# Two V tiles of a decode kernel loaded as 112 rows and two times 8 rows

## The chip, the core and the metric

The kernel runs on one core of a Trainium2 chip. The metric is the time of one execution on the device in microseconds (us). Three runs of the kernel before gave 1982.34, 1982.47 and 1984.11 us, median 1982.47 us.

## What is computed

The reference is one decode step through four attention layers. The token is a row `x` of 640 numbers. Each layer normalises `x`, multiplies it by `wq` to get 32 query heads of 192 numbers, scores every head against 8192 cached keys, takes the softmax, sums the 8192 cached values with it, multiplies the result by `wo` and adds it to `x`. Layers one and three use the caches and weights of set A, layers two and four those of set B. All data are bfloat16.

```
scores = einsum("bhqd,bhkd->bhqk", q, k_cache) * (Dh ** -0.5)
p = softmax(scores);  o = einsum("bhqk,bhkd->bhqd", p, v_cache)
x = x + o.reshape(B, Sq, H * Dh) @ wo
```

Each cache holds 32 x 8192 x 192 numbers, about 100 MB, and there is one query row for all of it: nearly all the work is to bring K and V in once per layer.

## The kernel before

**Tiles.** Heads are taken two at a time, as 16 pairs `p` per layer (index `l` from 0, so layers two and four are `l` = 1 and 3). The K or V of one pair is laid over 128 partitions, each with 128 cached rows of 192 numbers: 49,152 bytes in a partition, 6144 KB in a tile. `pool` has eight slots of half a tile (`TS` elements per partition). A transfer that `whole` (L210) allows fills two neighbouring slots with one `dma_start` (L379); others fill one slot (L381), and the last V of layers two and four comes as a half and two quarters (L374, L375).

**Compute.** For each pair, `products` (L589) lets VectorE multiply K by the query in place (L599, four pieces per half) and TensorE sum the products with a held identity matrix (L612). `softmax` (L616) reduces, finds the maximum and takes the exponential. `values` (L641) lets TensorE sum V with the probabilities (L678) into `OY`; L664 is the wait for the V tile. `gather` (L688) collects the sums on VectorE (L696, L697) and TensorE (L710). At the end of a layer the last V, `gather`, and the projection by `wo` (`project`, L531, or `project_row`, L563) must be through before the next layer's query can be formed.

**Order.** The program is written out by hand: `steps` is the order of the compute, `plan` the order of the loads. All large loads are issued by the sync engine (SP), in the order of `plan`, on one queue. `ahead` (L404) issues the next load as soon as the steps that free its slot are written down; on the chip SP then waits for the semaphore of that step, and so an issue waits for the compute that empties its slot. Each slot has a semaphore, which a landed transfer raises by 16; `need` (L396) gives the event to wait for. A wait on an engine's own list that is already covered by an earlier one is left out (`Queue.wait`, L22).

**Around the change.** In layer two the V tile of pair index 11 is the transfer issued at 855.92 us of the profiled execution, behind a K tile issued at 850.79 us and ahead of the K tile issued at 864.85 us. In layer four the V tile of index 11 is issued at 1809.76 us and the next K tile at 1826.66 us.

Of the kernel before, what the change touches and what calls it, by code (L numbers as in the profile page):

```python
# [61 lines left out]


PAIRS_W = 5
NSLOT = 8
KEPT = {0: {("k", 0)}, 1: {("v", 14), ("v", 15)}}


def build(nc, A_x, A_k, A_v, A_wq, A_wo, B_x, B_k, B_v, B_wq, B_wo, out):
    _, H, SK, DH = A_k.shape  # L70
    D = A_x.shape[-1]
    P = 128
# [13 lines left out]
    TS = JU * DH  # L86
# [11 lines left out]
    with ExitStack() as ctx:  # L98
# [6 lines left out]
        def sem(name):  # L105
            return ctx.enter_context(nc.semaphore(name))

        ident = sb("ident", [P, P], BF16)
        pool = sb("pool", [P, NSLOT * TS], BF16)
# [57 lines left out]
        PE = Queue(sem("pPE"))  # L167
# [2 lines left out]
        PO = Queue(sem("pPOOL"))  # L170
        SP = Queue()
        semS = [sem(f"semS{i}") for i in range(NSLOT)]
        semOL, semOE, semOB, semVQ, semX, semOUT = [sem(n) for n in ("semOL", "semOE", "semOB", "semVQ", "semX", "semOUT")]

        e = PO.op(lambda g: g.memset(ident[:], 0.0))
        PO.op(lambda g: g.affine_select(out=ident[:], in_=ident[:], compare_op=ALU.not_equal, fill=1.0,
# [5 lines left out]
        e = PO.op(lambda g: g.memset(mask, 0.0))  # L182
        for t in range(G):
            e = PO.op(lambda g, t=t: g.affine_select(
                out=mask, in_=mask, compare_op=ALU.not_equal, fill=1.0,
                base=-32 * t, pattern=[[-1, 2], [-2, VK]], channel_multiplier=1), e)
# [39 lines left out]
        for l in range(NL):  # L226
# [8 lines left out]
            for p in range(NPAIR):  # L235
# [17 lines left out]
                if p < NPAIR - 2:  # L253
                    if first_load("v", l, p) == (l, p):
                        plan += [("v", l, p, u) for u in range(2)]
                        if l == 2 and p == 1:
                            i = plan.index(("k", l, 1, 0))
# [4 lines left out]
                    if p + 1 in (PAIRS_W, 2 * PAIRS_W):  # L262
                        b = (p + 1) // PAIRS_W - 1
# [64 lines left out]
                    plan[i:i + 2] = [m, n]  # L328
                    turn[n[1:3]] = (1, 0)

        freed, landed = {}, {}
        issued = [0]

        def wq_rows(l, g):
# [10 lines left out]
        def transfer(n):  # L345
            l = n[1]
            o = ORDER[l]
            w = W[l % 2]
            free = [freed[b] for b in before[n]]
            if n[0] in ("wol", "woe"):  # L350
                r0 = o["wol"] * PD
                a, b = (0, OI) if l < 3 else (0, OI - 1) if n[0] == "wol" else (OI - 1, OI)
                return SP.op(lambda s: s.dma_start(
                    rows[:, a * D:b * D], w["wo"][r0:r0 + PD].rearrange("(p i) n -> p (i n)", p=P)[:, a * D:b * D]),
                    *free, sem=semOL if n[0] == "wol" else semOE, inc=16)
            if n[0] == "t":
                return max(free, key=lambda e: e[1]) if free else None
            if n[0] == "wob":
                r0 = o["wo"][2] * PD
                return SP.op(lambda s: s.dma_start(  # L360
                    slot[place[("wo", l, 2)]][:, (NW - NB[l]) * D:NW * D],
                    w["wo"][r0:r0 + PAIRS_W * PD].rearrange("(p i) n -> p (i n)", p=P)[:, (NW - NB[l]) * D:]),
                    sem=semOB, inc=16)
            if n[0] == "vq":
                n = ("v", l, NPAIR - 1, 1)
            i = place[n]
            t = slot[i]
            if n[0] in "kv":
                h = 2 * pair(l, n[2])
                r = w[n[0]][0, h:h + 2].rearrange("h (p j) d -> (h p) (j d)", j=J)  # L370
                if quarters(n):
                    x = TS // 2
                    if n in landed:
                        return SP.op(lambda s: s.dma_start(t[:, x:], r[:, TS + x:]), sem=semVQ, inc=16)  # L374
                    return SP.op(lambda s: s.dma_start(t[:, 0:x], r[:, TS:TS + x]), *free, sem=semS[i], inc=16)  # L375
                if whole(*n[:3]):
                    if n[3] == 1:
                        return landed[n[:3] + (0,)]
                    f = lambda s: s.dma_start(pool[:, i * TS:(i + 2) * TS], r)  # L379
                else:  # L380
                    f = lambda s: s.dma_start(t, r[:, n[3] * TS:(n[3] + 1) * TS])  # L381
            elif n[0] == "wq" and l < 2:
                f = lambda s: s.dma_start(pool[:, i * TS:i * TS + DC * QW], w["wq"].rearrange("(p c) n -> p (c n)", c=DC))
            elif n[0] == "wq":
                c0, k = Q_PARTS[n[2]]
                f = lambda s: s.dma_start(
                    wq_rows(l, n[2]),
                    w["wq"][:, o["q1"] * PD:o["q1"] * PD + QC].rearrange("(p c) n -> p c n", c=DC)[:, c0:c0 + k, :])
            else:
                r0 = o["wo"][n[2]] * PD  # L390
                k = NW - NB[l] if n[2] == 2 else NW
                f = lambda s: s.dma_start(
                    t[:, 0:k * D], w["wo"][r0:r0 + PAIRS_W * PD].rearrange("(p i) n -> p (i n)", p=P)[:, 0:k * D])
            return SP.op(f, *free, sem=semS[i], inc=16)

        def need(n):  # L396

            while n not in landed:
                m = plan[issued[0]]
                issued[0] += 1  # L400
                landed[m] = transfer(m)
            return landed[n]
# [45 lines left out]
        def layer(l, ev_z, ev_true):  # L448
# [7 lines left out]
            if l == 2:  # L456
                busy(2)
            e = DV.op(lambda v: v.scalar_tensor_tensor(out=nv[:], in0=mv[:, 0:1], scalar=mv[:, 0:1], in1=mv[:, 1:2],
                                                       op0=ALU.mult, op1=ALU.subtract))
            e = DV.op(lambda v: v.tensor_scalar(vs[:], nv[:], -float(DH), float(DH) * EPS, ALU.mult, ALU.add), e, last["rs"])  # L460
# [6 lines left out]
            if l < 2:  # L467
                e = need(("wq", l, 0))
# [4 lines left out]
            else:  # L473
                e = ev_first[l - 2]
# [166 lines left out]
            def values(p, us=(0, 1)):  # L641

                par = (l * NPAIR + p) % 2
                nl, np_ = first_load("v", l, p)
                k = 2 if p == NPAIR - 1 else VK
                N = min(512, k * DH)
                PE.wait(ev_p[p])
                if 0 in us:
                    PE.wait(last["rl"])
                    if p < NPAIR - 1:  # L650
                        e = PE.op(lambda t: t.matmul(TB[96:97, C_L:C_L + 2], lhsT=ones[:, 0:1], rhs=l_col[par][:],  # L651
                                                     start=True, stop=True), bank=TBu)
                    else:
                        for h in range(2):
                            e = PE.op(lambda t, h=h: t.matmul(TB[64 * h:64 * h + 64, C_L:C_L + 1], lhsT=ones[:, 0:1].broadcast_to([P, 64]),
                                                              rhs=l_col[par][:, h:h + 1], start=True, stop=True),
                                      signal=h == 1, bank=TBu)
                    last["lc"][par] = ev_l[p] = e
                PE.wait(last["O"])
                rounds = J // k // G  # L660
                for r in range(us[0] * rounds // 2, (us[-1] + 1) * rounds // 2):
                    u, i = divmod(r, rounds // 2)
                    u = turn[nl, np_][u]
                    PE.wait(need(("v", nl, np_, u)))  # L664
                    t = slot[place[("v", nl, np_, u)]]
                    if p == NPAIR - 1 and i == rounds // 4 and quarters(("v", nl, np_, u)):
                        if l == 3:
                            busy(6)
                        PE.wait(need(("vq", l)))
                    for c in range(k * DH // N):  # L670
                        for g in range(G):
                            j = (i * G + g) * k
                            o, x, y = (O[32 * g:32 * g + 2 * k, c * N:(c + 1) * N],
                                       p_sb[par][:, u * JU + j:u * JU + j + k, :].rearrange("p j h -> p (j h)"),
                                       t[:, j * DH + c * N:j * DH + (c + 1) * N])
                            f, fin = r == 0, r == rounds - 1
                            e = PE.op(lambda t, c=c, g=g, o=o, x=x, y=y, f=f, fin=fin: (
                                t.matmul(o, lhsT=x, rhs=y, start=f, stop=fin) if c == 0 else  # L678
                                matmul_held(t, o, x, y, f, fin, 32, 32 * g)),
                                signal=(fin and c == k * DH // N - 1 and g == G - 1), bank=Ou)  # L680
                if 1 not in us:
                    return
                ev_O[p] = last["p"][par] = e
                if not stays("v", l, p):
                    for u in range(2):
                        freed[("v", nl, np_, u)] = e
# [80 lines left out]
            if l + 1 == NL:  # L767
                a = slot[place[("wo", 3, 2)]][0:33, 0:HD]
                return a, AC.op(lambda c: c.activation(a, YR, ACT.Copy), ev_y, last["oT"], bank=YBu)
            ev_z = DV.op(lambda v: v.tensor_tensor(z[:], xc[:], YB[:, 0:DC], ALU.add), ev_y, ev_xc, bank=YBu)  # L770
            e = DV.op(lambda v: v.tensor_tensor(x_true[:], x_true[:], YB[:, 0:DC], ALU.add), ev_y, ev_true, bank=YBu)
# [60 lines left out]
```

## Time and profile before

| what | value |
|---|---|
| median of three runs | 1982.47 us (1982.34 to 1984.11) |
| span of the profiled execution, first to last instruction | 1982.1 us |
| bytes moved, mean rate over the span | 849.25 MB, 428 GB/s |
| DMA packets | 26,930; 12,416 of them of 49,152 bytes |
| busy: PE / DVE / ACT | 65% / 61% / 7% of the span |
| chain that ended last: DMA / DVE / PE | 67% / 17% / 15% |
| one `dma_start` at L379 on SP | 0.328 us |

The page gives no other time of the profiled execution than its span, which lies 0.4 us under the median of the runs. In the page, PE is TensorE, DVE is VectorE, ACT is ScalarE, SP is the sync engine. The core has 16 DMA engines that move the data; the DMA line gives the mean busy share of the 16 in each fortieth of the span, in tenths. A landing is told by 16 raises of its semaphore, and the trace holds the time of each raise; their spread tells how far the DMA engines are apart.

### The profile page before, as it was taken

What the parts mean: (1) busy time and instruction counts of PE and PEld (TensorE: products, weight loads), DVE (VectorE), ACT (ScalarE), POOL (GpSimd) and SP (SyncE); (2) the same over time, 40 slices, a digit from 0 to 9 for tenths busy, and PEclk for the clock granted to TensorE, in tenths of its full rate; (3) what the DMA queues carried; (4) which work ended last, traced back from release to release, by engine and by line L of the source; (5) the groups of instructions that cost most, each with busy time, mean ns of one, the idle gap of its engine ahead of it and who ended that gap; (6) DMA issues with size and microseconds to landing.
All of it is one profiled execution on the core that took longest, in us unless ns stands there. A gap on an engine that the chain in (4) does not pass through costs nothing.

```text
span 1982.1 us, 13748 instructions
## 1 busy us (share of the span) xinstructions
PE 1288.6 (65%) x8248; PEld 146.4 (7%) x3160; DVE 1201.2 (61%) x1376; ACT 139.9 (7%) x462; POOL 4.5 (0%) x23
## 2 busy tenths in 40 slices
PE   3567476666466666666785676675776766657658
PEld 0001001000100100100020010010001001000001
DVE  3566467467166657556745565665764775665656
ACT  0000000000000000000010000000000100000000
POOL 0000000000000000000000000000000000000000
PEclk9787776778677777777887877878787888777779
DMA  9999999999999999999999999999999999999998
GB/s 414 438 431 430 431 436 432 430 430 429 435 432 433 434 430 432 429 435 433 426 407 426 425 426 426 432 430 431 434 429 427 435 431 433 433 432 431 433 433 367
DMA packets 26930, 849.25 MB, mean 428 GB/s; under 512 B 3058, under 2 KB 3188, under 8 KB 3828
## 3 DMA queue, kind: packets, MB, share of 16 engines
q1 hardware_dynamic: 26724, 848.38, 99.6%
q8 instruction: 45, 0.74, 0.2%
q14 instruction: 17, 0.14, 0.0%
q10 hardware_dynamic: 144, 0.00, 0.0%
HBM read 848.36 MB, written 0.00 MB: 428 GB/s over the span
## 4 chain that ended last, share of the span: by engine, by line
DMA 67%; DVE 17%; PE 15%; ACT 1%; issue 0%; SPq 0%
DMA pool<-in_B_k_cache_dram 27%; DMA pool<-in_A_v_cache_dram 20%; DVE pool L599 15%; DMA pool<-in_A_k_cache_dram 14%; PE S L58 6%; DMA pool<-in_B_v_cache_dram 6%; PE OY L58 5%; PE OY L678 3%; DVE acc L697 1%; ACT p_sb L636 1%; DVE s_sb L621 1%; PE S L612 0%; DVE m_bf L623 0%; PE OY L538 0%; PE QM L626 0%
## 5 line engine op out<-in xcount | busy, mean ns | idle before, releaser
L599 DVE TENSOR_TENSOR pool<-pool,q_sb 128x3072 bf16<-128x3072 bf16 x512 | 861.1, 1753 | 229.5 <-DMA pool<-in_B_k_cache_dram 133.5
L58 PE MATMUL S<-pool,ident 128*128 128x512 bf16 x2944 | 789.5, 425 | 19.5 <-DVE pool L599 17.6
L710 PE MATMUL TB<-acc,small 128*1 128x192 f32 x240 | 82.7, 495 | 212.0 <-DVE acc L697 212.0
L58 PE MATMUL OY<-pool,p_sb 128*16 128x512 bf16 x1920 | 202.7, 498 | 0.0
L696 DVE TENSOR_SCALAR acc<-OY,small 128x192 f32<-128x192 f32 x64 | 26.7, 418 | 287.5 <-PE OY L58 256.3
L678 PE MATMUL OY<-pool,p_sb 128*16 128x512 bf16 (+1 forms) x1216 | 148.2, 495 | 69.5 <-DMA pool<-in_A_v_cache_dram 63.5
L612 PE MATMUL S<-pool,ident 128*128 128x512 bf16 x128 | 61.8, 483 | 201.3 <-DVE pool L599 201.2
L697 DVE SCALAR_TENSOR_TENSOR acc<-OY,small,acc 128x192 f32<-128x192 f32 x424 | 177.1, 418 | 14.9
L621 DVE TENSOR_REDUCE s_sb<-S 128x64 f32<-128x512 f32 x128 | 88.0, 688 | 69.7 <-PE S L58 69.7
L527 ACT ACTIVATE q_sb<-QM 128x192 bf16<-128x192 f32 x60 | 19.9, 331 | 944.0 <-PE QM L521 944.0
L721 ACT ACTIVATE rows<-TB,small 1x192 bf16<-1x192 f32 x120 | 43.2, 406 | 596.3 <-PE TB L710 596.3
L692 DVE RECIPROCAL small<-TB 1x2 f32<-1x2 f32 x64 | 11.2, 175 | 94.5 <-PE TB L651 75.3
L636 ACT ACTIVATE p_sb<-s_sb,small 64x128 bf16<-64x128 f32 x128 | 55.7, 435 | 161.2 <-DVE small L630 160.4
L612 PEld LDWEIGHTS S<-pool,ident 128*128 128x128 bf16 x128 | 12.9, 101 | 676.2 <-DVE pool L599 604.4
L651 PE MATMUL TB<-small,ones 128*1 128x2 f32 x120 | 11.4, 165 | 74.1 <-ACT p_sb L636 74.1
L678 PEld LDWEIGHTS OY<-pool,p_sb 128*16 128x16 bf16 (+1 forms) x1216 | 39.8, 107 | 217.3 <-issue 138.8
L626 PE MATMUL QM<-ident,m_bf 128*64 128x64 bf16 x128 | 14.0, 216 | 54.4 <-DVE m_bf L623 53.9
L710 PEld LDWEIGHTS TB<-acc,small 128*1 128x1 f32 x240 | 19.8, 101 | 310.8 <-DVE acc L697 284.0
L630 DVE TENSOR_REDUCE small<-QM 128x1 f32<-128x64 f32 x64 | 14.4, 225 | 35.2 <-PE QM L626 35.2
L521 PEld LDWEIGHTS QM<-rows,one_b 1*64 1x64 bf16 x120 | 6.2, 100 | 347.0 <-issue 341.1
L538 PE MATMUL OY<-oT,pool 128*128 128x1 bf16 x675 | 28.6, 178 | 1.9 <-ACT oT L584 1.9
L538 PEld LDWEIGHTS OY<-oT,pool 128*128 128x128 bf16 x675 | 27.8, 131 | 3.8 <-ACT oT L584 2.5
(74 smaller groups left out, 215.2 us busy)
## 6 DMA issues: line engine op xcount, KB each, us to landing
pool<-in_B_k_cache_dram SPq DMA_DIRECT2D x28, 6144.0 KB, 37.9
pool<-in_B_v_cache_dram SPq DMA_DIRECT2D x28, 6144.0 KB, 33.5
pool<-in_A_v_cache_dram SPq DMA_DIRECT2D x27, 6144.0 KB, 27.5
pool<-in_A_k_cache_dram SPq DMA_DIRECT2D x34, 3072.0 KB, 20.5
pool<-in_A_k_cache_dram SPq DMA_DIRECT2D x14, 6144.0 KB, 36.4
pool<-in_A_v_cache_dram SPq DMA_DIRECT2D x10, 3072.0 KB, 14.7
pool<-in_B_k_cache_dram SPq DMA_DIRECT2D x8, 3072.0 KB, 22.5
pool<-in_A_wo_dram SPq DMA_DIRECT2D x6, 2400.0 KB, 21.9
```

What stands on the lines that cost most here:

```text
L58: return t.add_instruction(mybir.InstMatmult(name=t.bass.get_next_instruction_name(), engine=mybir.EngineType.PE, ins=[t.lower_ap(rhs), t. ...
L527: lambda a: a.activation(q_sb[i][:], QM[:, 0:DH], ACT.Copy), e, last["q"][i], bank=QMu)
L538: e = PE.op(lambda t, i=i, c=c, f=y_first[0], fin=n[0] == "wol" and i == k - 1: t.matmul(YB[:, c:c + 1], lhsT=t3[:, i, c:D:DC], rhs=o[:, i ...
L599: e = DV.op(lambda v, d0=d0: v.tensor_tensor(k3[:, :, d0:d0 + QD], kin[:, :, d0:d0 + QD], q_sb[qi][:, d0:d0 + QD].unsqueeze(1).broadcast_t ...
L612: t.matmul(S[:, :], lhsT=ident[:], rhs=k3[:, :, d0:d0 + R], start=True, stop=fin) if d0 == 0 else
L621: lambda v, u=u: v.tensor_reduce(s[:, u * JU:(u + 1) * JU], SP_[u][:].rearrange("p (j r) -> p j r", r=R), AX.X, ALU.add), ev_S[p, u], last ...
L636: ev_p[p] = AC.op(lambda a, h=h, r=r: a.activation(p_sb[par][r, :, h], s[r, :], ACT.Exp, bias=negm[par][r, 0:1], accum_out=l_col[par][r, h ...
L678: t.matmul(o, lhsT=x, rhs=y, start=f, stop=fin) if c == 0 else
L696: v.tensor_scalar(acc[:], O[:, 0:DH], pick[:, 0:1], None, ALU.mult) if i == 0 else
L697: v.scalar_tensor_tensor(out=acc[:], in0=O[:, i * DH:(i + 1) * DH], scalar=pick[:, i:i + 1], in1=acc[:], op0=ALU.mult, op1=ALU.add)), e if ...
L710: e = PE.op(lambda t, h=h: t.matmul(TB[96:97, C_O + h * DH:C_O + (h + 1) * DH], lhsT=half[:, h:h + 1], rhs=acc[:], start=True, stop=True), ...
L721: last["TO"] = last["row_written"] = AC.op(lambda a, h=h: a.activation(orow[:, o0 + h * DH:o0 + (h + 1) * DH], TB[96:97, C_O + h * DH:C_O ...
```

## The change

In `transfer`, a whole tile that is listed in `ASIDE` no longer comes in one transfer of 128 rows. It comes as one of 112 rows (partitions 0 to 111) under the slot's semaphore, and, issued straight behind it by the same engine, two of 8 rows each (partitions 112 to 119 and 120 to 127) under a new semaphore `semA`. In `values`, TensorE waits for that semaphore too. The rows, their places and the bytes are the same. Two tiles are listed: V of pair index 11 in layers two and four.

```diff
+ASIDE = {("v", 1, 11), ("v", 3, 11)}
+ASIDE_ROWS = 16
...
-        freed, landed = {}, {}
+        freed, landed, aside = {}, {}, {}
...
                 if whole(*n[:3]):
                     if n[3] == 1:
                         return landed[n[:3] + (0,)]
-                    f = lambda s: s.dma_start(pool[:, i * TS:(i + 2) * TS], r)
+                    if n[:3] in ASIDE:
+                        a = P - ASIDE_ROWS
+                        e = SP.op(lambda s: s.dma_start(pool[0:a, i * TS:(i + 2) * TS], r[0:a]), *free, sem=semS[i], inc=16)
+                        for b in range(a, P, 8):
+                            aside[n[:3]] = SP.op(lambda s, b=b: s.dma_start(pool[b:b + 8, i * TS:(i + 2) * TS], r[b:b + 8]),
+                                                 sem=semA, inc=16)
+                        return e
+                    else:
+                        f = lambda s: s.dma_start(pool[:, i * TS:(i + 2) * TS], r)
...
-                    PE.wait(need(("v", nl, np_, u)))
+                    PE.wait(need(("v", nl, np_, u)), aside.get(("v", nl, np_)))
```

More of the change, by code (lines that the diff above doesn't have):

```diff
@@ L172, in build @@
         semS = [sem(f"semS{i}") for i in range(NSLOT)]
-        semOL, semOE, semOB, semVQ, semX, semOUT = [sem(n) for n in ("semOL", "semOE", "semOB", "semVQ", "semX", "semOUT")]
+        semOL, semOE, semOB, semVQ, semX, semOUT, semA = [
+            sem(n) for n in ("semOL", "semOE", "semOB", "semVQ", "semX", "semOUT", "semA")]
         e = PO.op(lambda g: g.memset(ident[:], 0.0))
```

## The prediction

> **What bounds the kernel.** I first read the slices of the page, its queues and the chain that ended last.
>
> ```profile
> DMA  9999999999999999999999999999999999999998
> GB/s 414 438 431 430 431 436 432 430 430 429 435 432 433 434 430 432 429 435 433 426 407 426 425 426 426 432 430 431 434 429 427 435 431 433 433 432 431 433 433 367
> ...
> q1 hardware_dynamic: 26724, 848.38, 99.6%
> q8 instruction: 45, 0.74, 0.2%
> ...
> DMA 67%; DVE 17%; PE 15%; ACT 1%; issue 0%; SPq 0%
> ```
>
> The DMA engines are busy from end to end, on one queue; the 17% and 15% of VectorE and TensorE in the chain lie beside running transfers. So time can be won only where DMA engines stand idle. The view of windows shows where: at the ends of layers two and four.
>
> ```profile
> 1002.00:1004.00 2.00, 1.72 (x24) 0.80 (x28) 0.00 (x0) 0.00 (x0) 0.00 (x0) 0.50 0.99 414
> 1004.00:1006.00 2.00, 2.00 (x31) 1.14 (x19) 0.00 (x0) 0.00 (x0) 0.00 (x0) 0.68 0.82 342
> 1006.00:1008.00 2.00, 1.72 (x43) 1.71 (x43) 0.17 (x1) 0.19 (x1) 0.00 (x0) 1.00 0.78 272
> ...
> 1972.00:1974.00 2.00, 2.00 (x26) 0.40 (x13) 0.00 (x0) 0.00 (x0) 0.00 (x0) 1.00 0.92 380
> 1974.00:1976.00 2.00, 0.88 (x18) 0.29 (x16) 0.00 (x0) 0.00 (x0) 0.00 (x0) 1.00 0.58 241
> 1976.00:1978.00 2.00, 1.77 (x23) 0.87 (x13) 0.84 (x2) 0.00 (x0) 0.00 (x0) 1.00 0.37 144
> ```
>
> The last two columns are the DMA share and GB/s. The share doesn't drop at once but over 4 to 6 us: some DMA engines have finished while others still work. The trace holds the 16 raises of a landing's semaphore, one per DMA engine. At 36 us they lie within 1.07 us. For the last V transfer of layer two the eighth engine is 2.99 us behind the first, the ninth 3.57, the last 6.35 (landed at 1009.58); in layer four 3.19, 4.13 and 6.10 (1975.38). Compute waits for the last one, as the chain shows:
>
> ```profile
> 993.05 16.54 DMA pool<-in_B_v_cache_dram
> ...
> 1937.43 37.95 DMA pool<-in_B_v_cache_dram
> ```
>
> Followed packet by packet, eight engines carry in turn the 16,384-byte packets of q8 (about 1.07 us each, 45 in the run), which fits a leading and a trailing eight. The trace doesn't number the engines.
>
> **What the change does to the load of the engines.** A row of 49,152 bytes is one packet: 12,416 such packets are 97 whole tiles of 128. A packet takes 1.82 us (trace median), so a tile costs each of the 16 engines 8 packets, 14.53 us from one tile to the next. The 112 rows can be 7 packets each, 12.7 us. A transfer of 8 rows has 8 packets, so at least eight engines get none of it. If the same eight take both, they carry 9 rows and the others 7. No transfer of before has fewer than 16 packets on q1 but the output's, so which engines these are isn't shown.
>
> **Costs beside other work.** SP issues two more transfers per listed tile, at the 328 ns of
>
> ```profile
> L379 SPq DMA_DIRECT2D pool<-in_B_v_cache_dram x28: 327/328/328, 531.1 to 1914.1; - x28
> ```
>
> that is 0.66 us before SP can wait for the next slot. Next in line is the K issue at 864.85 us, 8.9 us after 855.92; the transfer starts only after some 18 us more (first landing 897.54 minus 14.53), so the 0.66 us cost nothing. Without this cover they would cost 0.66 us each time. The added wait of TensorE at L664 stands before V's matmuls:
>
> ```profile
> 891.68 0.11 PEld L678 LDWEIGHTS OY<-pool,p_sb 128*16 128x16 bf16 x4
> ```
>
> In layer two V of index 11 has landed at 888.55 and is used at 891.68, a margin of 3.1 us (1855.12 and 1858.56 in layer four, 3.4 us). If the 8 rows land later than that, `gather` and the K issue at 896.17 move with TensorE; this issue's packets start at 912 (926.61 minus 14.53), so some 16 us of queued work cover it; in layer four the issue at 1863.07 has 30 us. So the wait by itself moves nothing; what counts is how far engines on q1 fall back.
>
> **The price of the 8-row transfers.** This is the unknown. Lower end: eight engines write eight rows side by side, 1.82 us. Upper end: eight neighbouring partitions take their rows one after another, 8 x 1.82 = 14.5 us, which is also the time in which any eight partitions get their rows in the rows of before (14.53 us a tile). Each row is near to one side of the question: the packet's is for an engine, the tile's is for a group of partitions. I see no reason to prefer one and take the middle, (1.82 + 14.53) / 2 = 8.2 us for each. The eight engines then need 12.7 + 2 x 8.2 = 29.1 us in place of 14.53, **14.5 us more**; at the ends +1.82 us, and 12.7 + 29.1 - 14.5 = +27.2 us.
>
> [...]
>
> **Forecast: slower, 2001 us.** I take the eight to be the leading ones. [...] Layer two: 0.6 + 14.5 = 15.1 in place of 6.35, +8.8 us. Layer four: 1.2 + 14.5 = 15.7 in place of 6.10, +9.6 us. The lag stays until an end of a layer, since the engines that are late always have queued work. Sum: 1982.1 + 18.4 = 2000.5 of span, and with the 0.4 us by which the median of the runs lies above it, 2001. Chance 0.60. Own range 1990 (a price of about 5.5 us per transfer: 12.7 + 11 - 14.5 = 9.2, less a lead of 5.3, is +4 each) to 2012 (the trailing eight take them, 2 x 14.5 = 29). With 14.5 us per transfer it would be +21 and +22, 2026; I give no more than 0.06 to the part above 2011.
>
> **Rival: a levelling (chance 0.25).** The 8 rows cost 1.82 us each and fall on the leading eight, which go back by one row while the trailing eight gain one. Layer two: the greater of 2.99 + 1.82 = 4.81 and 6.35 - 1.82 = 4.53, so 1.54 us are gained; layer four: 3.19 + 1.82 = 5.01 in place of 6.10, 1.09. Together 2.6 us, 1979.8: within 0.2% of the time, which is 3.96 us. This is the other side: not slower. It decides if an 8-row transfer takes less than about 3.5 us (the lead of the middle engine, 6.35 - 0.6 = 5.75 and 6.10 - 1.2 = 4.9 us, 5.3 on average, plus the spared row of 1.82 is 7.1 us for the two). For it: the two groups at 2.99 and 3.57. More than one row can't be won at either end, so 3.6 us is the limit, 1978.8.
>
> **Rival: the wrong eight (0.08).** As before, but the trailing eight take the rows: 1.82 us lost at each end, 3.6 together, 1986.1. For it: nothing in the trace names the engines.
>
> **Rival: no effect (0.07).** The rows go to the engines that would have had them anyway: two engines with four rows each per transfer. The load is as before, 1982.5.
>
> **How the numbers follow.** The likeliest is the price, 2001. About 0.2% is what a measurement of this kernel can tell from no change, so the bounds are 1978.5 and 1986.4. Faster than that needs a levelling beyond its limit, or other lags in the run: 0.04. Within: 0.21 of the levelling, 0.07 no effect, 0.05 of the wrong eight, 0.02 of a price that the lead just covers: 0.35. Slower: 0.61. The range goes from 1979 (leaving some 0.07 below) to 2011 (0.06 above).
>
> **What would show it.** Right: in the changed trace the packets of the 16 rows take far more than 1.82 us; the raises of the K tile behind (issued at 864.85) lie some 15 us apart and not 5.5; the DMA share falls off over 15 us at the end of layer two and of the run; the chain still ends on the V transfer. Wrong: packets of 1.82 us there and raises of the last V within about 5 us mean the levelling; raises 8 us apart mean the wrong eight. The forecast is wrong as well if the price is one or two rows, if half the rows fall on other engines, or if a late wait at L664 holds the queue empty.

## The result and the profile after

Four runs of the changed kernel took 2035.13, 2036.33, 2037.01 and 2040.3 us, median 2036.67; four of the kernel before on the same chip had a median of 1982.4. The ratio is 1.0276, with a 95% interval of 1.0262 to 1.0289: **slower by 54.3 us**. The profiled execution is the one of 2035.13 us; its span is 2033.3 us, 51.2 more than before.

The page of the changed kernel: DMA share in tenths, GB/s in 40 slices of 50.8 us, the queue, and the chain that ended last.

```profile
DMA  9999999999999999999999999999999999999998
GB/s 417 432 433 431 432 433 428 433 434 432 433 433 432 429 432 433 430 226 432 423 396 429 427 432 435 427 429 436 428 428 434 433 432 433 433 430 346 309 433 356
...
q1 hardware_dynamic: 26756, 848.38, 99.5%
...
DMA 61%; PE 19%; DVE 16%; another core or an unknown queue 2%; ACT 1%; issue 1%; SPq 0%
```

The rate tells where the time went: 226 in the eighteenth slice (864 to 915 us) and 346 and 309 in the 37th and 38th (1830 to 1932), against 430 or so around them. These are the two listed tiles. The DMA line above it stays at nines throughout: the engines count as busy while each packet takes longer. Two other slices are low, 396 and the last, 356; they were 407 and 367 before, and layers two and four end there.

The windows of that stretch (start and end in us, length, busy time of PE, PEld, DVE, ACT and POOL, granted clock, DMA share, GB/s), first before the change:

```profile
868.00:880.00 12.00, 5.36 (x17) 0.40 (x5) 6.37 (x5) 0.72 (x2) 0.00 (x0) 0.57 0.98 422
880.00:892.00 12.00, 9.15 (x51) 0.42 (x11) 9.39 (x10) 1.31 (x5) 0.00 (x0) 1.00 1.02 442
892.00:904.00 12.00, 5.58 (x52) 0.89 (x16) 4.32 (x10) 0.72 (x2) 0.00 (x0) 0.67 0.98 422
```

and after it:

```profile
868.00:880.00 12.00, 0.99 (x4) 0.13 (x1) 0.98 (x1) 0.72 (x2) 0.00 (x0) 0.50 1.10 246
880.00:892.00 12.00, 10.73 (x42) 0.20 (x2) 12.00 (x8) 0.00 (x0) 0.00 (x0) 0.85 0.98 217
892.00:904.00 12.00, 2.36 (x14) 0.30 (x6) 2.44 (x6) 1.31 (x5) 0.00 (x0) 0.72 1.12 172
904.00:912.00 8.00, 0.00 (x0) 0.00 (x0) 0.00 (x0) 0.00 (x0) 0.00 (x0) 0.50 0.82 166
912.00:924.00 12.00, 4.81 (x52) 0.80 (x20) 3.34 (x8) 0.36 (x2) 0.00 (x0) 0.76 0.94 393
```

The rate halves at 868.9 us, when the first DMA engine starts on the 112 rows, long before the 8-row transfers. It falls further, to 166 to 172, when these come, and is back by 915. By single packets: from 868.9 us on **all 16 engines** are slow, those still on the K tile before included. A packet of 49,152 bytes that starts between 870 and 891 us takes 3.0 to 3.8 us, most of them 3.5 to 3.8, in place of 1.82; one that starts between 891 and 910, with the 8-row transfers under way, takes 3.7 to 6.3 us. Added up over the whole run, the packets take 49.6 us longer for each of the 16 engines, out of the 51.2 us by which the span grew. So nearly all of the loss is slow packets, and at most 1.6 us are a queue left empty by the late wait, which the prediction named as one more way to be wrong. The K tile behind (issued at 863.90) lands at 929.26, against 903.08 before: 26.2 us later. Its raises are 8.59 us apart, 5.54 before.

The loss is not won back, and not enlarged, at the ends of the layers. The windows there after the change:

```profile
1028.00:1030.00 2.00, 1.37 (x32) 0.67 (x32) 0.00 (x0) 0.00 (x0) 0.00 (x0) 1.00 0.96 407
1030.00:1032.00 2.00, 1.72 (x35) 1.61 (x32) 0.17 (x1) 0.18 (x1) 0.00 (x0) 1.00 0.89 371
1032.00:1034.00 2.00, 2.00 (x51) 1.79 (x53) 0.00 (x0) 0.00 (x0) 0.00 (x0) 0.93 0.96 346
2024.00:2026.00 2.00, 2.00 (x24) 0.36 (x9) 0.00 (x0) 0.00 (x0) 0.00 (x0) 1.00 0.69 265
2026.00:2028.00 2.00, 1.55 (x20) 0.39 (x17) 0.43 (x2) 0.00 (x0) 0.00 (x0) 1.00 0.18 76
```

The last V of layer two lands at 1036.03 us (1009.58 before, +26.4) with its raises 6.51 us apart (6.35 before); that of layer four lands at 2026.62 (1975.38, +51.2) with raises 9.45 apart (6.10). So the second tile costs another 24.8 us, and all of it is still there at the end.

The chain of waits (start, us, what) has these three lines:

```profile
896.84 18.13 another core or an unknown queue
...
1889.52 17.85 another core or an unknown queue
...
1989.53 37.09 DMA pool<-in_B_v_cache_dram
```

The first two have no name, but the timeline (start, busy us, instruction, idle time before and what ended it) gives one to the first:

```profile
915.11 0.61 PE L689 MATMUL OY<-pool,p_sb 128*16 128x512 bf16 x4 [18.27 <-DMA pool<-in_B_v_cache_dram]
```

It is TensorE at the added wait for the 8 rows (the V matmuls are L689 now). Compute stands there, but the queue still has packets: the next K tile is issued at 919.14, and its own packets start only at 935 (first landing at 949.74, less 14.53). The transfers behind it are late by themselves. The third line shows that the run still ends on a V transfer.

### The profile page after: what moved, and what is told of

It reads as the page before. It is cut to its first block, busy times and chain, and to the rows that moved or that the text cites. A ratio compares the mean times of both kernels' runs of the same rounds, so it can differ in the third digit from the quotient of the medians.

```text
span 2033.3 us, 13754 instructions
## 1 busy us (share of the span) xinstructions
PE 1291.3 (64%) x8248; PEld 146.6 (7%) x3160; DVE 1201.1 (59%) x1376; ACT 139.8 (7%) x462; POOL 4.5 (0%) x23
## 4 chain that ended last, share of the span: by engine, by line
DMA 61%; PE 19%; DVE 16%; another core or an unknown queue 2%; ACT 1%; issue 1%; SPq 0%
DMA pool<-in_B_k_cache_dram 24%; DMA pool<-in_A_v_cache_dram 19%; DMA pool<-in_A_k_cache_dram 15%; DVE pool L610 13%; PE S L58 9%; PE OY L58 5%; DMA pool<-in_B_v_cache_dram 4%; PE OY L689 3%; DVE acc L708 1%; ACT p_sb L647 1%; DVE s_sb L632 1%; PE S L623 1%; PE OY L549 0%; DVE m_bf L634 0%
## 5 line engine op out<-in xcount | busy, mean ns | idle before, releaser
L58 PE MATMUL S<-pool,ident 128*128 128x512 bf16 x2944 | 789.9, 425 | 20.0 <-DVE pool L610 18.6
L689 PE MATMUL OY<-pool,p_sb 128*16 128x512 bf16 (+1 forms) x1216 | 146.8, 491 | 101.3 <-DMA pool<-in_A_v_cache_dram 59.2
L732 ACT ACTIVATE rows<-TB,small 1x192 bf16<-1x192 f32 x120 | 43.1, 405 | 628.5 <-PE TB L721 628.5
L689 PEld LDWEIGHTS OY<-pool,p_sb 128*16 128x16 bf16 (+1 forms) x1216 | 39.1, 106 | 250.9 <-issue 176.3
## 6 DMA issues: line engine op xcount, KB each, us to landing
pool<-in_A_v_cache_dram SPq DMA_DIRECT2D x10, 3072.0 KB, 15.1
```

The lines of the kernel that those rows point to most:

```text
L58: return t.add_instruction(mybir.InstMatmult(name=t.bass.get_next_instruction_name(), engine=mybir.EngineType.PE, ins=[t.lower_ap(rhs), t. ...
L732: last["TO"] = last["row_written"] = AC.op(lambda a, h=h: a.activation(orow[:, o0 + h * DH:o0 + (h + 1) * DH], TB[96:97, C_O + h * DH:C_O ...
```

## The experiments

Each diff is against the changed kernel; what differs is the list of tiles and the branch that loads them. `d` is the tile in `pool`, `r` its rows in the cache. Where a tile comes in several transfers, the first raises the slot's semaphore, the others `semA`, and TensorE waits for both, as in the change. Times are single runs, but where an interval is given; beside them stands a run of the kernel before on the same chip, or the median of 13 where 1982.49 is named. The four runs of the changed kernel lie 5 us apart, so less than that between two single runs shows nothing.

**One transfer of 16 rows.** Is it the 8-row form that costs?

```diff
-                        for b in range(a, P, 8):
-                            aside[n[:3]] = SP.op(lambda s, b=b: s.dma_start(pool[b:b + 8, i * TS:(i + 2) * TS], r[b:b + 8]),
...
+                        parts = [(a, a) for a in (slice(0, 112), slice(112, 128))]
...
+                        for a, b in parts:
+                            g = lambda s, a=a, b=b: s.dma_start(d[a], r[b])
```

The first entry of a pair is the place in the tile, the second the rows of the cache. The next experiments with several transfers of rows differ from this one in `parts` and, where it is shown, in the list of tiles.

> The 16 rows come in one transfer instead of two of 8, the 112 rows as in the change, in both tiles. [...] Theory two (the 8-row transfers are the whole cost, as the prediction had it): the 112 rows run at 1.82 us per packet and the time is within a few us of before, under 1990 us.

Measured: 2028.58 us against 1982.59, +46.0, or 23.0 per tile. The windows:

```profile
880.00:892.00 12.00, 10.23 (x39) 0.20 (x2) 12.00 (x8) 0.00 (x0) 0.00 (x0) 0.79 0.94 205
892.00:904.00 12.00, 3.08 (x17) 0.30 (x6) 3.16 (x6) 1.31 (x5) 0.00 (x0) 0.78 1.14 193
```

The rate is halved just as long. Joining the two 8-row transfers saves 4 us a tile (27.1 less 23.0), not most of the price: the price isn't that of the 8-row form alone. Theory two (under 1990 us) is out.

**Two transfers of 64 rows.** Here every engine gets 4 rows of each transfer, if rows are shared out evenly, and no transfer is small.

```diff
+                        parts = [(a, a) for a in (slice(0, 64), slice(64, 128))]
```

> The two listed tiles come as two transfers of 64 rows, partitions 0 to 63 and 64 to 127. [...] A rival theory, that only a row count that is no power of two is handled badly (112): packets of 1.82 us and no change, 1982 us.

Measured: 2025.68 us, +43.1, or 21.5 per tile. One window of its stretch:

```profile
880.00:892.00 12.00, 9.55 (x33) 0.20 (x2) 11.37 (x7) 0.00 (x0) 0.00 (x0) 0.68 0.99 213
```

Half rate through the whole tile, 3.4 to 4.4 us per packet on all 16 engines. The 1982 us expected for a row count that is a power of two did not come. It isn't an uneven number of rows per engine, on which the prediction was built. It isn't smallness either: a cut at partition 64 is enough.

**Eight neighbouring rows, or eight rows apart.** The tile of layer two alone comes in 16 transfers of 8 rows, once of neighbouring partitions, once of partitions four apart.

```diff
-ASIDE = {("v", 1, 11), ("v", 3, 11)}
+ASIDE = {("v", 1, 11)}
...
+                        parts = [(a, a) for a in [slice(b, b + 8) for b in range(0, P, 8)]]
```

for the neighbouring rows, and for those four apart

```diff
+                        parts = [(a, a) for a in [slice(h + b, h + b + 29, 4) for h in range(0, P, 32) for b in range(4)]]
```

> Layer two only: the listed tile comes as 16 transfers of 8 neighbouring rows each; layer four as in the kernel before. [...] A rival theory, that any short transfer halves the rate whatever its partitions: packets of 3.6 us, 58 us for the tile, about +38 us, near 2020 us. Engines at their own rate (1.82 us per packet, 29 us): +9 us, 1991 us.

> As the kernel with 16 transfers of 8 neighbouring rows, layer two only, but the 8 rows of a transfer lie 4 partitions apart (the same rows of the tile to the same partitions, in another order). [...] If the partitions do not matter: the same time as that kernel.

Measured: neighbouring 2033.62 us, +51.0; four apart 2016.13, +33.5, both for one tile. Windows of the neighbouring rows:

```profile
868.00:880.00 12.00, 1.44 (x4) 0.34 (x4) 0.50 (x2) 0.72 (x2) 0.00 (x0) 0.50 1.09 250
880.00:892.00 12.00, 9.70 (x37) 0.20 (x2) 11.93 (x8) 0.00 (x0) 0.00 (x0) 0.80 0.95 262
...
904.00:916.00 12.00, 0.00 (x0) 0.00 (x0) 0.00 (x0) 0.00 (x0) 0.00 (x0) 0.50 0.99 168
```

and of the rows four apart:

```profile
868.00:880.00 12.00, 5.58 (x17) 0.45 (x5) 6.39 (x5) 0.72 (x2) 0.00 (x0) 0.57 1.00 430
...
892.00:904.00 12.00, 0.00 (x0) 0.00 (x0) 0.00 (x0) 0.00 (x0) 0.00 (x0) 0.52 1.01 209
904.00:916.00 12.00, 0.00 (x0) 0.00 (x0) 0.00 (x0) 0.00 (x0) 0.00 (x0) 0.50 0.99 209
```

The 430 is the most telling figure of the study. Eight-row transfers run at full rate (1.82 us per packet) into the lower 64 partitions when their rows lie four apart, and at half rate (3.5 to 3.9 us) as soon as the same pattern goes to the upper 64. Neighbouring rows take 3.4 to 4.5 us for the first 10 us, then 2.6 to 2.9 in the lower half and 4.6 to 4.8 in the upper. Neither 2020 nor 1991 us, the times expected for them, came out; and the rows four apart took 17.5 us less than they did, so the partitions do matter. So eight rows in a transfer need not cost anything by their number; it depends on which partitions they go to. In every slow stretch the slow packets are on all 16 engines, though an 8-row transfer feeds eight: the others carry the ordinary tiles in front and behind and go just as slowly. The raises of the rows' semaphore also tell which eight these are. In the run with rows four apart, in the order in which the 16 engines end the K tile, they are the second, third, fourth, sixth, seventh, tenth, twelfth and fifteenth: five of the leading eight, three of the trailing.

With 16 short transfers, slow packets are not the whole price. The eight engines that get none of the V tile run out of work while TensorE waits for it, as the DMA share shows for the rows four apart:

```profile
916.00:928.00 12.00, 4.82 (x48) 0.60 (x16) 0.75 (x2) 0.00 (x0) 0.00 (x0) 0.56 0.58 197
```

Over the whole run (durations of all packets, divided by 16, against the span) the packets take 37.8 us longer than before with neighbouring rows and 19.4 four apart; the engines stand idle 11.9 and 12.8 us longer. So the partitions are compared by the rates and the packets, not by the whole price of a tile.

**Rows eight apart in the lower half.** As the one before, but in the lower 64 partitions the eight rows of a transfer lie 8 apart and so reach from 0 to 63. Do only rows that lie close together slow each other?

```diff
+                        parts = [(a, a) for a in [slice(b, b + 57, 8) for b in range(8)] + [slice(64 + h + b, 64 + h + b + 29, 4) for h in (0, 32) for b in range(4)]]
```

> [...]

Measured: 2029.4 us against 1982.49, +46.9, where four apart gave +33.5. In the lower half:

```profile
868.00:880.00 12.00, 1.44 (x4) 0.34 (x4) 0.63 (x2) 0.72 (x2) 0.00 (x0) 0.50 1.11 242
```

242 in place of 430 GB/s, 3.6 to 3.8 us per packet, but some of 2.1 to 3.2 between 882 and 888. Packets take 34.1 us longer in all, against 19.4 four apart. No two of the eight rows are closer than eight partitions, so it isn't only rows close together that go slowly; why those eight apart do isn't shown.

**Neighbouring partitions, rows apart in HBM.** Is it where the rows land or where they are read? The partitions are those of the neighbouring case; the cached rows are read four apart.

```diff
+                        parts = [(slice(h + 8 * b, h + 8 * b + 8), slice(h + b, h + b + 29, 4)) for h in range(0, P, 32) for b in range(4)]
```

> Layer two only: 16 transfers of 8 rows to neighbouring partitions, but their rows in HBM lie 4 apart, so 128 rows of this V tile land on other partitions than their probabilities and the sum over this tile is changed. If the partitions set the cost: as with neighbouring rows, 2034 us, packets of 2.8 us and then 4.6. If the place in HBM sets it: as with rows 4 apart, 2016 us, packets of 1.82 and then 3.8.

Measured: 2040.05 us, +57.6, against +51.0 with the rows read side by side. Windows:

```profile
868.00:880.00 12.00, 1.44 (x4) 0.34 (x4) 0.77 (x2) 0.72 (x2) 0.00 (x0) 0.53 1.09 242
...
904.00:916.00 12.00, 0.00 (x0) 0.00 (x0) 0.00 (x0) 0.00 (x0) 0.00 (x0) 0.50 1.07 168
```

Spreading the reads gains nothing; the rates are those of the neighbouring case or somewhat lower (156 against 172 GB/s from 916 to 928). The rows four apart have the same reads in the same order and differ from this kernel in the partitions alone: 2016.13 against 2040.05. The partitions decide. Whether the reads add a little to it, the 6.6 us more are too few to tell.

**The 112 rows alone.** The 8-row transfers are left out in both tiles, and with them the added wait.

```diff
-                        for b in range(a, P, 8):
...
+                        return SP.op(lambda s: s.dma_start(pool[0:a, i * TS:(i + 2) * TS], r[0:a]), *free, sem=semS[i], inc=16)
```

> Both tiles: only the 112 rows are loaded, the 16 rows of the two short transfers are left out (the sum over these tiles is changed). If the 112 rows run at half rate by themselves: about 25 us each in place of the 12.7 at full rate and 14.5 of the whole tile, +11 us per tile, near 2004 us, so that of the 54 us some 22 are due to them and 32 to the 8-row transfers. If the 112 rows are slow only because short transfers stand behind them: packets of 1.82 us and 1979 us.

Measured: 2012.91 us, +30.4, or 15.2 per tile, with an eighth of the tile's bytes gone; the 112 rows are slow by themselves. Its windows:

```profile
880.00:892.00 12.00, 10.10 (x39) 0.20 (x2) 12.00 (x8) 0.00 (x0) 0.00 (x0) 0.82 0.98 213
892.00:904.00 12.00, 3.01 (x17) 0.30 (x6) 3.09 (x6) 1.31 (x5) 0.00 (x0) 0.75 0.94 213
```

More than half of the 27.1 us per tile is the large transfer; the two small ones add the other 11.9 us, some 1.8 of it for the bytes that are missing here. An estimate comes near the 15.2: all engines are slow from the first one's entry into the tile to the last one's exit, some 7 packets and 5.4 us of spread (3 packets), so 10 packets cost 1.82 us more each, 18.2, less the 1.82 us of the row left out: 16.4.

**The same work cut by columns.** Three transfers again, with the same sizes, the same extra issues, semaphore and wait, but each spans all 128 partitions: 112, 8 and 8 of the 128 cached rows that a partition holds.

```diff
+                        for a, b in ((0, 112), (112, 120), (120, 128)):
+                            g = lambda s, a=a * DH, b=b * DH: s.dma_start(d[:, a:b], r[:, a:b])
```

> Both tiles in three transfers with the same two extra issues, the same second semaphore and the same waits as the change, but cut along the 128 numbers of rows within a partition (112, 8 and 8), so that each transfer has all 128 partitions. If the cost lies in the partitions: no change, 1982 to 1984 us, packets of 48 KB cut into 43 and 3 KB at the usual rate. If the issues, the waits or the number of transfers cost: a part of the 54 us is seen here.

Measured in three rounds: median 1983.23 us, ratio 1.0003 with an interval of 0.9994 to 1.0013. The windows, and the GB/s of the page:

```profile
880.00:892.00 12.00, 9.12 (x48) 0.44 (x11) 9.50 (x9) 1.31 (x5) 0.00 (x0) 1.00 1.02 432
892.00:904.00 12.00, 5.87 (x54) 0.84 (x20) 4.04 (x10) 0.72 (x2) 0.00 (x0) 0.67 1.00 430
```

```profile
GB/s 413 437 432 429 430 434 430 434 431 429 436 430 432 431 434 431 428 433 432 429 408 426 430 432 430 432 431 427 433 430 428 433 433 432 434 431 431 432 430 371
```

No slice is low but the first and those at the ends of layers two and four, as before. Issues, semaphore and wait cost nothing that can be measured; TensorE doesn't stand at the wait here: it is busy for 5.87 us from 892 to 904, 5.58 before, 2.36 with the change. What is left for the 54 us is the cut across partitions.

**The 112 rows in layer one.** The branch is that of the 112 rows alone. Does the price of a tile follow from how far the engines are apart? In layer one they have drifted apart less (2.3 us in the run before, against 5.5 and 5.3 at the two tiles of the change), so a tile should cost less.

```diff
-ASIDE = {("v", 1, 11), ("v", 3, 11)}
+ASIDE = {("v", 0, p) for p in range(4, 8)}
```

> Only the 112 rows are loaded, in four V tiles of layer one (index 4 to 7) instead of the two of layers two and four; their 16 rows are left out, so the sums over these tiles are changed. There the 16 DMA engines are 2.3 us apart, against some 5.4 at the tiles of the change. If all engines run at half rate from the first engine's entry into the 112 rows to the last one's exit, a tile costs (7 rows + 2.3 / 1.82 rows) x 1.82 us less the 1.82 us of the row left out, 13.2 us, four of them 53 us: near 2035 us. If the cost doesn't depend on how far the engines are apart, it is the 15.2 us per tile of the kernel with 112 rows alone: near 2043 us.

Measured: 2023.64 us against 1981.76, +41.9 for four tiles, 10.5 each. The GB/s of its page:

```profile
GB/s 414 430 431 314 293 302 433 429 433 433 433 430 434 429 433 433 431 431 431 434 403 418 430 426 432 427 429 427 430 428 425 436 431 433 432 433 431 431 433 372
```

The direction holds, the size doesn't: neither 2035 nor 2043 us. With the engines 2.3 us apart at first the packets take some 3.2 to 3.8 us at the start and end of a tile but 2.0 to 3.0 in its middle. So a 112-row transfer isn't simply at half rate: a tile cost 15.2 us in layers two and four, 10.5 in layer one. The formula above is an estimate that fits one drift; on what the price depends, these two don't show.

**The change in layer two alone.**

```diff
-ASIDE = {("v", 1, 11), ("v", 3, 11)}
+ASIDE = {("v", 1, 11)}
```

> The change in layer two only. If each tile has its own price and nothing is won back later, half of the 54 us: near 2010 us. If a part of the loss of layer two is caught up in layers three and four (queued work, or a reset of the engines' lag at the end of layer two), the price of this one tile is less than half: under 2007 us, and that of layer four is the larger one.

Measured: 2009.24 us, +27.5, half of 54.3 within the spread of single runs. The two prices add up, and a loss in layer two is neither won back nor doubled later.

## Why the prediction was wrong in size

The direction was right, and in part for the reason given: which partitions a transfer writes sets how fast its rows come, 430 GB/s with rows four apart in the lower half and 242 eight apart. Why isn't shown. The forecast was +18.6 us; measured were 54.3.

**The step that failed first: "The 112 rows can be 7 packets each, 12.7 us."** It put the large transfer at the full rate, for no other reason than that each engine gets fewer rows. The 112 rows alone cost 15.2 us per tile over a whole tile of 14.5, that is 29.7 in place of 12.7. I asked how many rows an engine has, never which partitions the transfer writes; that question was put to the 8-row transfers only.

**The second: that only the engines with the 8 rows fall back, and their lead covers some of it.** "I take the eight to be the leading ones" gave back 5.3 us on average. The eight were five of the leading and three of the trailing where they could be told, and it doesn't matter, since packets were slow on all 16 engines (3.0 to 3.8 us from 870 to 891 us): none kept its 1.82 us while the others fell back. This also speaks against the levelling, beside the measured time. The 0.6 and 1.2 us in the sums, and in the lead of 5.3, stand for the middle of the leading eight: the mean of the fourth and fifth raise of the last V before. That the eight fall back together from that point was an assumption, which no run shows; the last raises came 6.51 and 9.45 us behind the first, not 15.1 and 15.7.

**The 8-row price was near by luck.** I took 8.2 us for each, the middle of two ends between which I could not choose; the two together add 11.9, 6.0 each. That number is what the 112 rows leave of the 27.1, so it adds up by construction and is no check of the sum. Against the 9.2 us per tile of the forecast (14.5 less the lead of 5.3), the 112 rows are 17.0 more, the two small transfers 4.5 less than 16.4, and the lead of 5.3 wasn't there: 27.0 us.

**What held.** The SP issues cost nothing and the wait by itself moves nothing: the cut by columns has both and is at 1.0003. The next K issue stayed covered, by 16 us in layer two; TensorE's 18 us at the wait lie inside the loss of the transfers, since slow packets alone are 49.6 of 51.2 us. The two tiles add up. The chain still ends on the V transfer, and the 8-row packets take far more than 1.82 us.

**The signs that I named misled.** Raises of the K tile 8 us apart should have meant the wrong eight, and 3.6 us; they were 8.59 apart, and the loss was 26 us: as packets were slow on all 16 engines, the spread grew by 3.05 us only while the K tile landed 26.2 later. The DMA share was to fall off over 15 us at the end of layer two and of the run; the raises there are 6.51 and 9.45 us apart. In the slow stretch it lay at 0.8 to 1.1, because the packets themselves took longer. The sign to look at was GB/s.

**What stays open.** That the partitions decide is shown by pairs of runs: columns against rows, four apart against eight apart, and the same reads to partitions four apart and to neighbouring ones. How they do isn't shown. In the upper half rows four apart have the same pattern as in the lower and go at half rate, 209 GB/s in place of 430. The lower half always came first, so no run tells the upper half from the later transfers. Neither is it shown why packets are slow on all 16 engines at once, nor why neighbouring rows cost 2.6 to 2.9 us in one half and 4.6 in the other. No run pointed to a version faster than the kernel before.

## What to carry to other kernels

Where DMA is the bound, cut a large load by columns, so that every transfer spans all 128 partitions: three transfers in place of one cost nothing here (ratio 1.0003), while every cut across partitions that was tried cost 10 to 58 us for a tile of 14.5 (11 to 14 of it idle engines in the cuts into 16). When a few rows are moved, price the large transfer that remains before the small ones. Read GB/s beside the DMA share: with the change the engines looked busy, a share of 0.98 from 880 to 892 us, at 217 GB/s.

## What the runs showed of the hardware

- A transfer of 112 or of 64 neighbouring partitions slowed the packets of all 16 engines, also of those on another transfer: mostly 3.5 to 3.8 us for 49,152 bytes in place of 1.82 with 112 rows, 3.4 to 4.4 with 64.
- With transfers of eight rows under way, the core moved 430 GB/s, the full rate, into partitions of the lower half that lie four apart, 242 eight apart, and 209 four apart in the upper half.
- The DMA share stayed near 1.0 while the rate fell to 213 GB/s with the 112 rows alone and to 168 with neighbouring rows.
